# Two usual pairs in place of four in the first gated block, and a re-ordered output stage

## The chip, the core and the metric

The kernel runs on one core of one Trainium2 chip. The metric is the device time of one execution in microseconds. The engines of the core are TensorE (PE in the profile, with PEld for its weight loads), VectorE (DVE), ScalarE (ACT), GpSimd (POOL) and SyncE (SP), which issues DMAs. Each engine works through its own instructions in order; semaphores make one engine wait for another or for a DMA. PE writes its products into PSUM, which has eight banks of 512 fp32 columns.

## What is computed

Two equal layers, each an attention part and a gated part with a residual around each. There are 2048 tokens of 448 features, 16 heads of 28 and 1792 hidden features.

```python
def _A_ref(x, wqkv, wo):
    q, k, v = ...                       # x @ wqkv, by heads
    scores = einsum("bhqd,bhkd->bhqk", q, k) * (Dh ** -0.5)
    o = einsum("bhqk,bhkd->bhqd", softmax(scores), v)
    return heads_together(o) @ wo

def _B_ref(x, w_gate, w_up, w_down):
    h = sigmoid(x @ w_gate) * (x @ w_up)
    return h @ w_down

x = A_x
x = x + _A_ref(_layernorm(x), A_wqkv, A_wo)
x = x + _B_ref(_layernorm(x), B_w_gate, B_w_up, B_w_down)
x = x + _A_ref(_layernorm(x), A_wqkv, A_wo)
x = x + _B_ref(_layernorm(x), B_w_gate, B_w_up, B_w_down)
```

## The kernel before

A layer runs through four stages: `project` (queries, keys, values), `attend`, `out_project` (the product with `wo` and the residual) and `gated`. The tokens stand in 16 tiles of 128, and four tiles make a block of 512. In the products of these stages every fp32 operand is split into two fp16 parts, high and low, and a product is three matmuls: high by high, high by low, low by high. The order of the instructions on each engine is written out by hand; nothing is scheduled later.

**The output stage (`out_project`, L1365).** For a token tile, `products` (L1373) runs nine matmuls of 448 columns into one bank, and `tails` (L1376) adds the last 64 features of the contraction; two tiles' second tail matmuls use halves of the array. `add` (L1387) adds the result into `x` on DVE. The tiles go in groups of 6, 4, 4 and 2. Block 0 is normalised meanwhile: `stats` (L493) on DVE and POOL, `scale` (L319) on DVE, then `turn_raw` (L511) transposes its four tiles on PE into the banks 4 to 7, ACT copies them to SBUF, and the nine `half_steps` (L385) make from them the fp16 operands `xwide` and `xshort`: sums and differences of quarters of the block, as a product in the manner of Strassen needs them.

**The gated stage (`gated`, L1463).** The outer loop runs over four blocks, the inner one over seven pairs of hidden tiles (`seq`). `gate_and_up` (L1610) computes for one pair the gate and the up product, 78 matmuls of 256 columns, in two PSUM tiles `chain` and two `side`. ACT copies partial sums out of `chain` (L1625); DVE adds `side` to them (L1641, `c11_c22`), after which PE goes on accumulating in `side` (`c12`, the last ten matmuls of the pair). Between these pieces stand six slots, `along(0)` to `along(5)`; `portions` (L1801) says how many steps of a queue `steps` are taken in which slot of which pair. The third slot, `along(2)`, is the last before `c11_c22`.

**The down product.** From block 1 on it runs a block late, in seven products a pair (`pieces`, L1556), each of six matmuls of 224 columns (L1552); `Operands` (L1495) makes their fp16 operands from the hidden values on ACT and DVE. For block 0, the first `USUAL` pairs take another way: `hidden` (L1695) splits the hidden values as they are, and `down` (L1587) runs 24 matmuls of 448 columns (L1600 to L1602) into four banks of their own, one pair later. `add_usual` (L1605) adds these banks into `x` at the pairs that `AFTER_USUAL` names. `load_usual` (L1439) loads the weights of this form, `load_dn` (L1447) those of the other, for block 0 only the pairs that are not usual.

**Blocks 1 to 3 before their use.** A block goes through a queue of steps (`steps`, L373). `norm_two` makes the statistics of two tiles (DVE) and their factors (POOL); `lift` scales a tile on ACT; `square` transposes it in squares of 32 on DVE. The last `square` also runs `store` (L342), four DMAs to a scratch in DRAM, and `gather` (L354), two DMAs back that bring the features onto the partitions (`xraw`). The nine `half_steps` follow; the first, `r11`, reads the gathered tile on DVE (L403) and on ACT (L411). All DMAs of `store` and `gather`, the usual weights and the first down weights are issued by SP, in order; the gate and up weights of a pair (1.6 MB, L1437) by POOL when PE has ended the pair two before.

Of the kernel before, what the change touches and what calls it, by code (L numbers as in the profile page):

```python
# [21 lines left out]
D = 448  # L22
# [3 lines left out]
NT = S // P  # L26
NB = 4
TB = NT // NB
# [28 lines left out]
N_SUMS = 25  # L57
DN = D // 2

AFTER_USUAL = ((0, 5), (0, 5), (1, 0), (1, 2))  # L60
N_DN = 8
USUAL = 4
SHORT = ((10, 23, 12), (11, 24, 13), (8, 22, 9))


# [53 lines left out]
def interleaved_layers(ctx: ExitStack, tc: tile.TileContext, x_in, wqkv, wo, w_gate, w_up,  # L119
                       w_down, out):  # L120
    nc = tc.nc
# [10 lines left out]
    banks = {"pool": None, "stack": None}  # L132
# [11 lines left out]
    def psum(tag, name, shape):  # L144
        uid[0] += 1
        return banks["pool"].tile(shape, F32, name=f"{name}_{uid[0]}", tag=tag, bufs=1)
# [4 lines left out]
    def bank(i, name):  # L151
        return psum(f"bank{i}", name, [P, 512])


    x = cpool.tile([P, NT, D], F32, name="x")
# [14 lines left out]
    back = cpool.tile([P, 4], F32, name="back")  # L170
# [92 lines left out]
    class Block:  # L263
# [246 lines left out]

        def turn_raw(self):  # L511
            self.turned = True
            self.turn_banks(4, range(4))
            self.raw = big.get("xraw", [P, 4, W])
            nc.gpsimd.memset(self.raw[64:P, 3, :], 0.0)
            for j in range(TB):
                self.turn(j)
            for kt, pt in self.pt.items():
                n = P if kt < 3 else 64
                nc.scalar.copy(self.raw[0:n, kt, :], pt[0:n])  # L520
            big.put(self.xn)
# [60 lines left out]
    def by_tokens(pm, hi, lo, tail, w, kts=range(4)):  # L582

        for kt in kts:
            if kt == 3:
                nc.tensor.matmul(pm, tail, w[:, 0, 3, :], start=False, stop=False)
                nc.tensor.matmul(pm, tail, w[:, 1, 3, :], start=False, stop=True)
                continue
            nc.tensor.matmul(pm, hi(kt), w[:, 0, kt, :], start=(kt == 0), stop=False)  # L589
            nc.tensor.matmul(pm, hi(kt), w[:, 1, kt, :], start=False, stop=False)  # L590
            nc.tensor.matmul(pm, lo(kt), w[:, 0, kt, :], start=False, stop=False)  # L591
# [114 lines left out]
    def run_fill(fill, n=1):  # L706
        for _ in range(n):
            if fill:
                fill.popleft()()
# [215 lines left out]
    class Measure:  # L925
# [27 lines left out]
        def add(self):  # L953
            kind, t, n = self.rows.popleft()
            m, n = {"o": (3, n), "d": (6, n), "gu": (4, 1024)}[kind]
            v = t[:, 0:n]
            junk = big.get("junk", [P, 2048], BF16)
            nc.vector.tensor_tensor_reduce(junk[:, 0:n], v, v, 1.0, sums[:, m:m + 1],
                                           op0=ALU.mult, op1=ALU.add,
                                           accum_out=self.part[:, 0:1])  # L960
            big.put_next(junk)
            nc.vector.tensor_copy(sums[:, m:m + 1], self.part[:, 0:1])
            if kind == "gu":
                junk = qrt.get("junk", [P, 1024], BF16)
# [29 lines left out]
    class Prepare:  # L994
# [119 lines left out]
        def split(self, raw, kind, j):  # L1114
# [22 lines left out]
            else:  # L1137
                n = N_DN if j < USUAL else N_DN - 1
                t = big.at(self.packs, "pack", [P, N_DN, 2, DN], F16)
                s12, s34 = [qrt.get("sums", [P, 2, DN]) for _ in range(2)]  # L1140
                b11, b12, b21, b22 = [v[:, z, c:c + DN] for z in (1, 0) for c in (0, DN)]
                for to, a, b in ((s12[:, 0], b12, b11), (s12[:, 1], b22, s12[:, 0]),
# [3 lines left out]
                         (t[:, 3:6:2], v[:, 0].rearrange("p (c n) -> p c n", c=2))]  # L1146
                if j < USUAL:
                    parts.append((t[:, 7], b12))
# [8 lines left out]
    class Outputs:  # L1157
# [9 lines left out]
        def hi(self, t):  # L1167
            return lambda kt: self.kt[kt][:, 0, t * P:(t + 1) * P]

        def lo(self, t):  # L1170
            return lambda kt: self.kt[kt][:, 1, t * P:(t + 1) * P]
# [193 lines left out]
    def out_project(outs, gate):  # L1365
        new_banks()
        nc.scalar.activation(warm, warm, AF.Sigmoid)
        nc.scalar.reg_load(gate_scale, back.bitcast(I32)[0:1, 3:4])
        first = Block(0, True)
        steps = deque([first.turn_raw] + first.half_steps())  # L1370
        early = 6

        def products(pm, t):  # L1373
            by_tokens(pm, outs.hi(t), outs.lo(t), None, gate.out, range(3))

        def tails(pms, ts):  # L1376


            for t in ts:
                nc.tensor.matmul(pms[t], outs.tail(t), gate.out[:, 0, 3, :], start=False,  # L1380
                                 stop=False)
            for i, t in enumerate(ts):
                r = slice(64 * (i % 2), 64 * (i % 2) + 64)
                nc.tensor.matmul(pms[t], outs.tail(t, i % 2), gate.out[r, 1, 3, :], start=False,  # L1384
                                 stop=True)

        def add(pm, t):  # L1387
            nc.vector.scalar_tensor_tensor(x[:, t, :], pm, back[:, 1:2], x[:, t, :],
                                           op0=ALU.mult, op1=ALU.add)

        gate.load_gu()
        gate.load_usual()
        pms = {t: bank(t, "op")[:, 0:D] for t in range(early)}
        for t in range(early):
            products(pms[t], t)
        first.begin()
        tails(pms, range(early))
        for t in range(early):
            add(pms[t], t)
            if t < TB:  # L1400
                first.stats(t)
            if t >= TB:
                first.scale(t - TB)
        for j in range(early - TB, TB):
            first.scale(j)
        for ts in (range(6, 10), range(10, 14), range(14, NT)):
            for t in ts:
                pms[t] = bank((6, 7, 0, 1, 2, 3, 4, 5, 0, 1)[t - early], "op")[:, 0:D]
                products(pms[t], t)
                if t >= 10:  # L1410
                    run_fill(steps, {10: 4}.get(t, 1))
            tails(pms, ts)
            for t in ts:
                add(pms[t], t)
        big.put(*outs.kt, gate.out)
        run_fill(steps, 9)
        return first


    class WeightsGated:  # L1420
# [18 lines left out]
        def load_usual(self):  # L1439

            self.usual = [big.get("usual", [P, 2, 4, 2, DN], F16)
                          for _ in range((USUAL + 1) // 2)]
            for p in range(USUAL):
                for i, k in enumerate((3, 5, 0, 7)):
                    nc.sync.dma_start(self.usual[p // 2][:, p % 2, i], dn_parts[k, :, p])

        def load_dn(self, queue=nc.sync):  # L1447
            t = big.get("dn", [P, NP, 2, DN], F16)
            first = USUAL if len(self.products) > NP * (NB - 1) else 0
            queue.dma_start(t[:, first:], dn_parts[self.products.popleft(), :, first:])  # L1450
# [12 lines left out]
    def gated(layer, first, wt, before_next):  # L1463
# [2 lines left out]
        low, high = slice(0, W // 2), slice(W // 2, W)  # L1466

        seq = [(b, p) for b in range(NB) for p in range(NP)]
        blks = [first] + [Block(b, True) for b in range(1, NB)]
        s1, s2 = blks[1].steps(), blks[2].steps()  # L1470
        norms = TB // 2
        ahead = norms + 2 * TB
        steps = deque(s1[:ahead] + s2[:norms] + s1[ahead:] +
                      s2[norms:ahead])
        banks_of = {}


# [65 lines left out]
        def of_block(b):  # L1543
            return range(USUAL if b == 0 else 0, NP)

# [157 lines left out]
        for b, p in seq:  # L1703
# [25 lines left out]
            for i, n in enumerate(portions(b, p)):  # L1729
                at[i].append(lambda n=n: run_fill(steps, n))  # L1730
            for j in range(TB):
                if AFTER_USUAL[j] == (b, p):
                    at[0].append(lambda j=j: add_usual(j))


            if b > 0:
                some = [q for q in (0, 1, 6, 2, 3, 4, 5) if q in of_block(b - 1)]
                for q in some:
                    i = {0: 0, 1: 1, 6: 2, 2: 3, 3: 4}.get(q, 5)
# [28 lines left out]
        b = NB - 1  # L1768
# [10 lines left out]
        for k in TAIL[3:]:  # L1779
            if k == 6:  # L1780
                for j, i in enumerate((0, 2)):
# [4 lines left out]
                    if last:  # L1786
                        t = b * TB + j
# [13 lines left out]
    def portions(b, p):  # L1801

        if b == 0:
            steps = {0: {1: 2, 2: 2, 4: 2, 5: 4}, 2: {1: 1, 2: 1, 5: 1},
                     3: {1: 1, 2: 1, 3: 1, 4: 1, 5: 1}, 4: {1: 1, 2: 1, 3: 2, 4: 2, 5: 2},
                     5: {1: 2, 2: 1}}
        elif b == 1:
            steps = {1: {1: 1, 5: 1}, 2: {5: 1}, 3: {2: 1}, 4: {1: 1, 5: 1}, 5: {1: 1, 5: 1},
                     6: {2: 1}}
        elif b == 2:  # L1810
            steps = {0: {1: 1, 2: 1}, 1: {1: 2, 2: 2, 5: 4}, 3: {5: 1}, 4: {1: 1, 2: 1, 5: 1},
                     5: {1: 1, 2: 1, 5: 1}, 6: {1: 1, 3: 1}}
        else:
            steps = {0: {1: 1, 2: 1}, 1: {1: 2, 2: 2, 5: 2}, 2: {1: 1, 2: 1, 5: 1},
                     3: {1: 1}, 4: {1: 1, 2: 1}, 5: {1: 2, 2: 2}, 6: {1: 2, 2: 2, 5: 2}}
        return [steps.get(p, {}).get(i, 0) for i in range(6)]
# [6 lines left out]
    first = Block(0)  # L1823
# [82 lines left out]
```

## Time and profile before

| | us |
|---|---|
| median of three runs | 1895.12 (1894.42 to 1895.16) |
| span of the profiled execution | 1893.0 |
| output stage of layer 0 | 565.9 to 600.3 |
| block 0 of layer 0's gated stage, pair 0 begins | 600.3 |
| output stage of layer 1 | 1501.7 to 1536.1 |
| block 0 of layer 1's gated stage, pair 0 begins | 1536.1 |

No time of its own is listed for the profiled execution beside its span; the median lies 2.1 us above the span.

In the timelines a row gives the start, the length, the engine, the line, the operation, what it writes and reads, and how many such instructions are merged in it; the brackets at its end give how long the engine had stood idle and who released it. A queue's own rows, with the letter q, are DMAs being issued. Matmuls overlap in the array, so their cost is the step from one start to the next and not the length. In a table of windows each engine has its busy time and, in brackets, its number of instructions; then come the clock of PE, the share of the DMA engines and GB/s. In the list of waits stand the total, the count and the longest. Line numbers are those of the kernel before.

### The profile page before, as it was taken

The numbers are of one execution on the slowest core, as the hardware profiler recorded it, in microseconds if no ns is written. First come the engines' busy times: TensorE is split into PE (matmuls) and PEld (weight loads), VectorE is DVE, ScalarE is ACT, GpSimd is POOL, SyncE is SP. The second block draws the span as 40 slices with busy tenths as digits, with TensorE's granted clock in tenths as the row PEclk, the third lists the DMA queues.
The fourth block names the chain that finished last, engine by engine and source line by source line (L and its number), as shares of the span: only waits on it lengthen the run. The fifth ranks groups of instructions, "written<-read, shape, count | busy, mean of one in ns | idle before, by whom it ended". The sixth has DMA issues, their size and how long they took to land. (4 is left out here: it accounts for less than half of the span.)

```text
span 1893.0 us, 56282 instructions
## 1 busy us (share of the span) xinstructions
PE 1886.5 (100%) x24254; PEld 1323.1 (70%) x24254; DVE 1430.7 (76%) x2835; ACT 1382.7 (73%) x1772; POOL 231.5 (12%) x453
## 2 busy tenths in 40 slices
PE   9999999999999999999999999999999999999999
PEld 4455555555556799999954556667666567999998
DVE  7758989898976688787564487787778676887664
ACT  5569999999993566555345799999999745565541
POOL 3023112222101111111100000000000020121110
PEclk9999999999999999999999999999999999999999
DMA  7676454334323566646734322122120245666553
GB/s 247 194 212 166 132 137 128 107 119 129 103 88 121 192 205 235 231 181 238 251 96 134 90 52 47 32 52 52 31 48 24 67 160 174 218 251 223 208 208 142
DMA packets 110882, 270.86 MB, mean 143 GB/s; under 512 B 13214, under 2 KB 67838, under 8 KB 110496
## 3 DMA queue, kind: packets, MB, share of 16 engines
q0 software_dynamic: 31776, 158.51, 23.4%
q1 hardware_dynamic: 78288, 108.20, 20.3%
q8 instruction: 192, 3.15, 0.7%
q10 hardware_dynamic: 560, 0.46, 0.1%
q14 instruction: 66, 0.54, 0.1%
HBM read 207.88 MB, written 50.85 MB: 137 GB/s over the span
## 5 line engine op out<-in xcount | busy, mean ns | idle before, releaser
L1222 ACT ACTIVATE prob_s<-sc 128x1536 f32<-128x1536 f32 (+1 forms) x657 | 887.9, 1487 | 6.6 <-PE sc L1207 5.9
L1258 PE MATMUL acc<-prob_s,val_s 128*32 128x256 f32 (+3 forms) x7700 | 569.9, 383 | 0.0
L1207 PE MATMUL sc<-qp_s 114*32 114x512 f16 x7868 | 553.2, 379 | 0.0
L579 PEld LDWEIGHTS <-gu_s 128*128 128x128 f16 x4368 | 426.9, 98 | 46.8 <-issue 0.4
L1207 PEld LDWEIGHTS <-qp_s 114*32 114x32 f16 x8192 | 272.7, 95 | 203.4 <-issue 88.3
L1258 PEld LDWEIGHTS acc<-prob_s,val_s 128*32 128x32 f32 x7700 | 272.3, 110 | 142.9 <-issue 13.6
L579 PE MATMUL chain<-xwide_s,gu_s 128*128 128x256 f16 x2016 | 247.5, 273 | 0.0
L1552 PE MATMUL dnp<-dn_s,hparts_s 128*128 128x224 f16 x2016 | 225.2, 259 | 0.0
L1552 PEld LDWEIGHTS <-hparts_s 128*128 128x128 f16 x2016 | 194.0, 98 | 4.4
L1238 DVE SCALAR_TENSOR_TENSOR power_q<-power_q,expo_q 128x512 f32<-128x512 f32 x243 | 168.2, 692 | 8.3
L1625 ACT COPY one_q<-chain 128x256 f32<-128x256 f32 x224 | 82.4, 371 | 121.4 <-PE chain L579 120.8
L1641 DVE TENSOR_TENSOR one_q<-side,one_q 128x512 f32<-128x512 f32 x112 | 72.2, 686 | 101.8 <-PE side L579 101.5
L579 PE MATMUL side<-xshort_s,gu_s 128*128 128x256 f16 x1120 | 140.5, 273 | 0.0
L564 PE MATMUL qkp<-xhl_s,wqk_s 128*128 128x512 f16 x616 | 138.1, 379 | 0.7 <-ACT wqk_s L231 0.2
L564 PEld LDWEIGHTS <-wqk_s 128*128 128x128 f16 x616 | 60.1, 98 | 69.8 <-ACT wqk_s L231 1.1
L1437 POOL DMA_DIRECT2D gu_s<-gu_parts x104 | 56.0, 538 | 430.5 <-PE side L579 424.5
L1287 DVE STREAM_TRANSPOSE oturned_q<-acc 128x512 f32<-128x512 f32 x32 | 22.9, 716 | 97.1 <-PE acc L1258 96.9
L1258 PE MATMUL acc<-power_q,val_s 128*32 128x256 f32 (+3 forms) x300 | 94.2, 396 | 0.0
L579 PE MATMUL side<-xwide_s,gu_s 128*128 128x256 f16 x672 | 91.6, 273 | 0.0
L1505 ACT CAST hparts_s<-hsums_q 128x256 f16<-128x256 f32 (+1 forms) x136 | 65.0, 494 | 30.2 <-DVE hsums_q L1517 20.2
L756 ACT ACTIVATE qkhl_q<-qkp 128x512 f16<-128x512 f32 x56 | 33.2, 593 | 71.9 <-PE qkp L564 68.3
L1652 ACT ACTIVATE one_q<-one_q 128x512 f32<-128x512 f32 x56 | 35.2, 629 | 64.3 <-DVE one_q L1641 64.3
(218 smaller groups left out, 2318.0 us busy)
## 6 DMA issues: line engine op xcount, KB each, us to landing
gu_s<-gu_parts POOLq DMA_DIRECT2D x104, 800.0 KB, 6.0
dn_s<-dn_parts POOLq DMA_DIRECT2D x42, 784.0 KB, 7.8
qp_s<-qk_scr SPq DMA_DIRECT2D x96, 224.0 KB
qk_scr<-qkhl_q SPq DMA_DIRECT2D x56, 256.0 KB
gu_parts<-pack_s POOLq DMA_DIRECT2D x14, 800.0 KB, 3.8
xt_scr<-xs_s SPq DMA_DIRECT2D x48, 224.0 KB
xraw_s<-xt_scr SPq DMA_DIRECT2D x12, 768.0 KB
qp_s<-qk_scr SPq DMA_DIRECT2D x64, 112.0 KB
```

Source lines behind the costliest of these rows:

```text
L564: nc.tensor.matmul(pm, w, x, start=(i == 0), stop=(i == len(terms) - 1))
L579: nc.tensor.matmul(pm, a, x, start=(first and i == 0), stop=(i == len(terms) - 1), skip_group_check=True)
L1207: nc.tensor.matmul(ps[32 * j:32 * j + 32, :], hd.k[:, keys], hd.q[:, qb * W:(qb + 1) * W], start=True, stop=True, tile_position=(0, 32 * j))
L1222: nc.scalar.activation(prob[:, 0:n, :], ps[:, 0:n, :], AF.Exp, scale=exp_scale)
L1238: nc.vector.scalar_tensor_tensor(p, p, c[k], y, op0=ALU.add, op1=ALU.mult)
L1258: nc.tensor.matmul(acc[qb * VC:(qb + 1) * VC, s], v[:, kc % TB, h, :], probs[c * NB + qb][:, s], start=(kc == 0 and a == 0), stop=(kc == N ...
L1437: queue.dma_start(self.gu[-1][m], gu_parts[p, m])
L1505: nc.scalar.copy(to[:, :, 0], a)
L1552: nc.tensor.matmul(pm, a[:, x, t], w[:, p, y], start=(begin and n == 0 and (j == 0 or alone)), stop=(n == 2), skip_group_check=True)
L1625: nc.scalar.copy(to, pm)
L1641: nc.vector.tensor_tensor(one[m], side[m], one[m], op=ALU.add)
L1652: nc.scalar.activation(out, v, AF.Sigmoid, scale=gate_scale)
```

## The change

Three things, in both layers.

- `USUAL` is 2: in block 0 the pairs 2 and 3 take the way of the seven products. `AFTER_USUAL` adds the first two banks at the pairs 3 and 4 of block 0. With it, `load_usual` loads half, `load_dn` five of seven pairs for block 0, from pair 1 on, and the preparation makes one part less for two pairs' down weights.
- The output stage takes the tiles in four groups of four tails. Block 0's tiles 0 to 3 are added and scaled first, and its transposition goes into the banks 2 to 5 behind the products of tiles 8 and 9.
- Block 1's two `norm_two` and four `lift` are made in the output stage, so its queue in the gated stage begins with the four `square`, the store and the gather. `portions` takes them in the second slot of pair 0, and `r11` in the third slot of pair 1. Before, the squares stood in the sixth slot of pair 0 and `r11` in the sixth of pair 2. The steps of block 2 that follow alternate between `lift` and `square`.

```diff
-AFTER_USUAL = ((0, 5), (0, 5), (1, 0), (1, 2))
+AFTER_USUAL = ((0, 3), (0, 4), (1, 0), (1, 2))
 N_DN = 8
-USUAL = 4
+USUAL = 2
...
         def turn_raw(self):
             self.turned = True
-            self.turn_banks(4, range(4))
+            self.turn_banks(2, range(4))
...
-        first = Block(0, True)
+        first, second = Block(0, True), Block(1, True)
         steps = deque([first.turn_raw] + first.half_steps())
-        early = 6
+        early = second.squared()[:TB + TB // 2]
+        pms = {}
...
-        pms = {t: bank(t, "op")[:, 0:D] for t in range(early)}
-        for t in range(early):
-            products(pms[t], t)
+        products(range(6), range(6))
         first.begin()
-        tails(pms, range(early))
-        for t in range(early):
-            add(pms[t], t)
-            if t < TB:
-                first.stats(t)
-            if t >= TB:
-                first.scale(t - TB)
-        for j in range(early - TB, TB):
-            first.scale(j)
-        for ts in (range(6, 10), range(10, 14), range(14, NT)):
-            for t in ts:
-                pms[t] = bank((6, 7, 0, 1, 2, 3, 4, 5, 0, 1)[t - early], "op")[:, 0:D]
-                products(pms[t], t)
-                if t >= 10:
-                    run_fill(steps, {10: 4}.get(t, 1))
-            tails(pms, ts)
-            for t in ts:
-                add(pms[t], t)
+        tails(range(4))
+        for t in range(4):
+            add(t)
+            first.stats(t)
+        products((6, 7), (6, 7))
+        tails(range(4, 8))
+        for t in range(4):
+            first.scale(t)
+        for t in range(4, 8):
+            add(t)
+        products((8, 9), (0, 1))
+        run_fill(steps)
+        for do in early[:2]:
+            do()
+        products((10,), (6,))
+        run_fill(steps, 2)
+        products((11,), (7,))
+        run_fill(steps)
+        tails(range(8, 12))
+        for t in range(8, 12):
+            add(t)
+        for do in early[2:]:
+            do()
+        products((12, 13), (2, 3))
+        run_fill(steps, 3)
+        products((14, 15), (0, 1))
+        run_fill(steps, 9)
+        tails(range(12, NT))
+        for t in range(12, NT):
+            add(t)
         big.put(*outs.kt, gate.out)
-        run_fill(steps, 9)
-        return first
+        return first, second
...
-        steps = deque(s1[:ahead] + s2[:norms] + s1[ahead:] +
-                      s2[norms:ahead])
+        steps = deque(s1[norms + TB:ahead] + s2[:norms] + s1[ahead:] +
+                      [s2[i] for i in (2, 6, 3, 7, 4, 8, 5, 9)])
...
         if b == 0:
-            steps = {0: {1: 2, 2: 2, 4: 2, 5: 4}, 2: {1: 1, 2: 1, 5: 1},
-                     3: {1: 1, 2: 1, 3: 1, 4: 1, 5: 1}, 4: {1: 1, 2: 1, 3: 2, 4: 2, 5: 2},
-                     5: {1: 2, 2: 1}}
+            steps = {0: {1: 4, 5: 2}, 1: {2: 1, 4: 1, 5: 2},
+                     2: {1: 1, 2: 1, 3: 1, 4: 1, 5: 3}, 3: {1: 2}, 4: {1: 2}, 5: {1: 2}}
```

More of the change, by code (lines that the diff above doesn't have):

```diff
@@ L1368, in out_project, with products, tails @@
         nc.scalar.reg_load(gate_scale, back.bitcast(I32)[0:1, 3:4])
-        first = Block(0, True)
+        first, second = Block(0, True), Block(1, True)
         steps = deque([first.turn_raw] + first.half_steps())
-        early = 6
-        def products(pm, t):
-            by_tokens(pm, outs.hi(t), outs.lo(t), None, gate.out, range(3))
-        def tails(pms, ts):
+        early = second.squared()[:TB + TB // 2]
+        pms = {}
+        def products(ts, banks):
+            for t, i in zip(ts, banks):
+                pms[t] = bank(i, "op")[:, 0:D]
+                by_tokens(pms[t], outs.hi(t), outs.lo(t), None, gate.out, range(3))
+        def tails(ts):
             for t in ts:
@@ L1385, in tails, with add @@
                                  stop=True)
-        def add(pm, t):
-            nc.vector.scalar_tensor_tensor(x[:, t, :], pm, back[:, 1:2], x[:, t, :],
+        def add(t):
+            nc.vector.scalar_tensor_tensor(x[:, t, :], pms[t], back[:, 1:2], x[:, t, :],
                                            op0=ALU.mult, op1=ALU.add)
@@ L1468, in gated @@
         seq = [(b, p) for b in range(NB) for p in range(NP)]
-        blks = [first] + [Block(b, True) for b in range(1, NB)]
+        first, second = first
+        blks = [first, second] + [Block(b, True) for b in range(2, NB)]
         s1, s2 = blks[1].steps(), blks[2].steps()
```

## The prediction

> **What bounds the kernel now.** I read the busy table of the page first, then the list of what TensorE (PE) waited for, then the timelines of the two changed stages, in layer 0 (565.9 to about 678 us) and in layer 1.
>
> ```profile
> span 1893.0 us, 56282 instructions
> ...
> PE 1886.5 (100%) x24254; PEld 1323.1 (70%) x24254; DVE 1430.7 (76%) x2835; ACT 1382.7 (73%) x1772; POOL 231.5 (12%) x453
> ```
>
> ```profile
> PE still L261 <- DVE warm L179: 1.3, 1, 1.3
> PE turn L508 <- DVE xn_s L320: 0.8, 1, 0.8
> PE qkp L564 <- ACT wqk_s L231: 0.2, 1, 0.2
> PE qkp L564 <- DVE xhl_s L543: 0.2, 1, 0.2
> ```
>
> These four rows are all of PE's waits on another engine, and all lie in the kernel's first 20 us. In the output stage and the gated block PE never waits: it runs one matmul after another, so their issue spacing sets the end there. Two consequences: work taken from PE is gained in full, but there is no wait to remove; and any wait that the change puts in front of PE is lost in full.
>
> **Part 1: fewer PE columns.** The pairs 2 and 3 of block 0 leave the usual form (24 matmuls of 448 columns a pair) for seven products of six 224-column matmuls (42 a pair).
>
> ```profile
> 1552.08 1.25 PE L579 MATMUL side<-xshort_s,gu_s 128*128 128x256 f16 x10
> 1557.71 1.47 PE L579 MATMUL chain<-xwide_s,gu_s 128*128 128x256 f16 x12
> ```
>
> ```profile
> 687.17 1.31 PE L1552 MATMUL dnp<-dn_s,hparts_s 128*128 128x224 f16 x12
> 688.32 1.47 PE L579 MATMUL chain<-xwide_s,gu_s 128*128 128x256 f16 x12
> ```
>
> Between the first two rows stand 10 matmuls of 256 columns (1.09 us, the step from 614.05 to 615.14 in a fence below) and one usual pair: 5.63 - 1.09 = 4.54 us. Twelve of 224 columns take 1.15 us, so 42 take 4.03. Gain: 0.51 us a pair, times two pairs and two layers: 2.06 us. That is the whole of what PE can gain, since the gate and up products do not change.
>
> What these pairs cost elsewhere: each drops two casts and two subtractions of 512 for seven casts, four sums and seven subtractions of 256. Row that covers it, from a pair that already works so:
>
> ```profile
> 675.61 1.29 DVE L1641 TENSOR_TENSOR one_q<-side,one_q 128x512 f32<-128x512 f32 x2 [0.92 <-PE side L579]
> ```
>
> VectorE (DVE) stands 0.92 us idle there; the new pairs 3 and 4 add a transposition (0.55) and an accumulator's addition (0.6), 1.15 in all, and the 0.28 us worked out in Part 3 absorbs the rest. I take 0; without this cover some 0.3 us a pair. Down weights of five pairs in place of three are loaded after pair 1 and not 3, on SyncE's (SP) queue behind the gather of Part 3, and are due only in block 1; the weights' preparation in attention makes two pieces fewer on DVE, which PE does not await. Both 0.
>
> **Part 2: the re-ordered output stage.** All matmuls stay, in four groups of tails of four token tiles each (before 6, 4, 4, 2).
>
> ```profile
> 576.13 1.30 PE L1380 MATMUL op<-wout_s,ot_s 128*128 128x448 f16 x6
> 577.36 0.74 PE L1384 MATMUL op<-wout_s,ot_s 64*128 64x448 f16 x6
> ...
> 584.86 0.92 PE L1380 MATMUL op<-wout_s,ot_s 128*128 128x448 f16 x4
> ...
> 586.19 0.36 PE L589 MATMUL op<-wout_s,ot_s 128*128 128x448 f16 x1
> ...
> 587.90 1.91 PE L508 MATMUL turn<-ident,xn_s 128*128 128x128 f32 x16
> ```
>
> ```profile
> 577.76 0.68 DVE L1388 SCALAR_TENSOR_TENSOR x<-op,back,x 128x448 f32<-128x448 f32 x1 [8.00 <-PE op L1384]
> ...
> 583.58 0.65 DVE L1388 SCALAR_TENSOR_TENSOR x<-op,back,x 128x448 f32<-128x448 f32 x1
> ...
> 585.17 1.35 DVE L320 TENSOR_SCALAR xn_s<-x,mv,rs 128x448 f32<-128x448 f32 x3
> 586.43 2.46 DVE L1388 SCALAR_TENSOR_TENSOR x<-op,back,x 128x448 f32<-128x448 f32 x4
> ```
>
> A group of four tails takes 1.33 us (584.86 to 586.19), two tiles' products 18 x 0.19 = 3.4. New order on PE from 576.13: tails to 577.46, products 6 and 7 to 580.9, tails to 582.2, products 8 and 9 to 585.6, then the transpositions. They now write banks 2 to 5, so bank 5 needs tile 5 added. DVE begins two tails (0.38) earlier, at 577.38; four additions with statistics take 5.82 (577.76 to 583.58), four scalings 1.7, two additions 1.25: 586.2. PE waits about 0.35 us for it, 0.7 in both layers. Bounds: 0 and 0.7 a layer (one addition more). The block's start moves with it: pair 0 begins at S0 = 600.28 + 0.35 = 600.63.
>
> Block 1's statistics (3.0 us on DVE), GpSimd's (POOL) eight small operations and ScalarE's (ACT) four scalings (2.8) now stand between block 0's transposition and its operands.
>
> ```profile
> 565.90:600.30 34.40, 34.40 (x197) 17.66 (x194) 23.24 (x43) 8.24 (x15) 3.64 (x9) 1.00 0.37 116
> ```
>
> In this stage DVE (23.24 of 34.40 us) and ACT (8.24) have room. Following their queues, block 0's wide operands are done by about 598 and its short ones by 601; PE needs the first at S0, the last in S0 + 5.2. Cost 0; DVE is the thinner cover, and a late operand would cost PE its delay one for one. On POOL's queue these stand ahead of weight loads that wait for pair 0's end anyway.
>
> **Part 3: block 1's trip through memory.** Its squares (four transpositions), the store (four DMAs on SP) and the gather (two) move from the end of pair 0 to its second slot, and the gather's first user, r11, from pair 2's last slot to pair 1's third. There r11's cast stands on ACT ahead of the sigmoids, and its subtractions on DVE ahead of the sums of side and one; both engines work in order. PE's last ten matmuls of pair 1 need these sums.
>
> ```profile
> 600.28 1.49 PE L579 MATMUL chain<-xwide_s,gu_s 128*128 128x256 f16 x12
> ...
> 608.81 1.47 PE L579 MATMUL chain<-xwide_s,gu_s 128*128 128x256 f16 x12
> ...
> 614.05 1.25 PE L579 MATMUL side<-xshort_s,gu_s 128*128 128x256 f16 x10
> 615.14 1.26 PE L579 MATMUL chain<-xshort_s,gu_s 128*128 128x256 f16 x10
> 616.23 1.26 PE L579 MATMUL side<-xshort_s,gu_s 128*128 128x256 f16 x10
> 617.32 0.35 PE L1600 MATMUL dnp<-usual_s,hhl_q 128*128 128x448 f16 x1
> ```
>
> ```profile
> 610.18 2.22 DVE L316 STREAM_TRANSPOSE xs_s<-lifted_q 128x448 f32<-128x448 f32 x4
> ...
> 615.21 1.29 DVE L1641 TENSOR_TENSOR one_q<-side,one_q 128x512 f32<-128x512 f32 x2 [1.32 <-PE side L579]
> ```
>
> ```profile
> 631.50 0.76 DVE L403 TENSOR_TENSOR t_q<-xraw_s 128x256 f32<-128x256 f32 x2
> ```
>
> When the data must be there: the second sum ends at 616.50, the second five matmuls start at 616.23 + 0.55, so the sums may start 0.28 late, 6.68 after the pair's start (608.81). Before them stand r11's subtractions, 0.76. So the gather must land 5.92 into pair 1, which starts 8.53 after S0: at S0 + 14.45.
>
> When the store starts: the last four additions begin as the last tails end (about S0 - 0.1, as at 577.76 against 577.36) and take 2.4, the squares 2.22: S0 + 4.5. The trip has 9.9 us. What it takes today:
>
> ```profile
> 65.58 3.43 SPq L349 DMA_DIRECT2D xt_scr<-xs_s  x4
> 73.73 0.38 SPq L357 DMA_DIRECT2D xraw_s<-xt_scr  x1
> ```
>
> ```profile
> 79.20 1.14 ACT L218 CAST xhl_s<-xraw_s 128x512 f16<-128x512 f32 x2 [4.75 <-DMA xraw_s<-xt_scr]
> ```
>
> ```profile
> 612.43 4.28 SPq L349 DMA_DIRECT2D xt_scr<-xs_s  x4
> 619.52 0.39 SPq L357 DMA_DIRECT2D xraw_s<-xt_scr  x1
> ```
>
> ```profile
> 1548.28 3.18 SPq L349 DMA_DIRECT2D xt_scr<-xs_s  x4
> ```
>
> ```profile
> 1567.24 0.71 ACT L411 CAST xwide_s<-xraw_s 128x256 f16<-128x256 f32 x2 [0.27 <-DMA xraw_s<-xt_scr]
> ```
>
> Two landings are seen, because an engine waited for them: 79.20 - 65.58 = 13.6 us, and 1567.24 - 1548.28 = 19.0 in layer 1, where the store met a weight load. From parts: the shorter store here (612.43 to 619.52, 7.1) with the gather of 73.73 (5.5) makes 12.6. None is near 9.9. In the new place the store starts while no weight load runs, as at 65.58, so I take 13.6: PE waits 13.6 - 9.9 = 3.7 us in each layer, 7.4 together; bounds 2.7 (12.6) and 9.1 (19.0) a layer. What is behind it: ACT's sigmoids and DVE's products of pair 1; PE then has a usual pair (4.54) to run, in which they catch up, so nothing more is late, and pair 3's weight load slips as PE does.
>
> The Trainium skill (DMA: Bandwidth & Descriptors, Anatomy of one DMA) fits a transfer with 2.0 us plus its bytes at 436 GB/s; with that, 0.9 MB out and 0.8 MB back would be an estimated 7.9 us, the wait would vanish and the sum be 1893.8. The trace's 13.6 disagrees.
>
> **Sum**, against the profiled span: 1893.0 - 2.06 + 0.7 + 7.4 = 1899.0, 6.0 more. The median of the runs lies 2.1 above that span, so 1895.1 + 6.0 = 1901.1 us.
>
> **Rivals.** (a) The trip fits into 9.9 us: not slower. For it: the SP queue has eight loads fewer ahead; a gather whose store meets nothing may beat 12.6. Against: no row does. It decides at 9.9: -2.06 + 0.7, 1893.8. (b) The collision of layer 1 stays: there the trip is 19.0 and the wait 9.1: -2.06 + 0.7 + 3.7 + 9.1 = +11.4, 1906.5. For it: the row itself; against: the store leaves some 7 us earlier, ahead of that load. (c) The new wait lets PE's clock fall back.
>
> ```profile
> 1.25 4.87 PE L261 MATMUL still<-still_q 128*128 128x512 f16 x11 [1.25 <-DVE warm L179]
> ...
> 10.54 0.59 PE L261 MATMUL still<-still_q 128*128 128x512 f16 x2
> 10.97 0.50 PE L626 MATMUL sums<-first_sums,ones 128*128 128x1 f32 x4
> ```
>
> At the start 11 matmuls of 512 need 4.87 us, later two need 0.43 (10.54 to 10.97): eleven at that pace are 2.4, so a cold spell costs about 2.5 us; 5.0 in two layers, 1906.1. Against: a wait of 3.7 may be too short. The Trainium skill (TensorE: Matmul & The Clock Gate, Part 1) lets the clock fall after an idle window of about 3.4 us that runs free of the kernel; by that, waits above 3.4 are at the threshold.
>
> **How the numbers follow.** Forecast 0.55, (a) 0.15, (b) 0.13, (c) 0.12; 0.05 for a gain that I do not see. A measurement of this kernel tells about 0.2% (3.8 us) from no change: (a) is within it, and so is the forecast's low end (12.6 gives 1899.0 and a little less falls inside), 0.05. So faster 0.05, same 0.20, slower 0.75. The range takes in (a) to (b): 1893.5 to 1906.5; the forecast's own is 1898 to 1904.
>
> **What would show it.** A row of ACT or DVE released by the gather in pair 1 of block 0, at L411 or L403, in both layers; a PE wait on DVE of 2.5 to 5 us before that pair's last ten matmuls; about 0.35 at the transpositions; a usual-form count of 96 matmuls a layer halved to 48. The prediction is wrong if PE still waits for nothing in pair 1, if the store leaves earlier than 4 us into pair 0, or if PE waits in pairs 2 to 6.

## The result, and the profile after

| | before | after |
|---|---|---|
| median of 11 runs, us | 1894.94 (1894.27 to 1896.11) | 1900.38 (1897.88 to 1903.09) |
| span of the profiled execution, us | 1893.0 | 1897.4 |

The ratio after to before is 1.0024 (95% interval 1.0017 to 1.0032): slower by 5.4 us. The profiled execution after took 1899.11 us and had the full clock, as 5 of the 11 runs did; it explains 4.4 us. The other six show a granted clock of 0.999 over the run, which comes below.

The list of PE's waits after has three rows beyond the kernel's first 20 us that the list before does not have (total, count, longest):

```profile
PE side L579 <- DVE one_q L1654: 4.1, 2, 2.1
...
PE turn L508 <- DVE x L1391: 0.5, 2, 0.3
...
PE vp L589 <- DVEq L901: 0.4, 1, 0.4
```

The last lies at 116.3 us, in the products for the values of layer 0, which the change leaves alone; before, PE loses 0.15 us there, so it counts for 0.2. The other two come twice, once a layer. The first, in the timelines of SP, ACT, DVE and PE of layer 0 (lines 1552 to 1641 of the kernel before are lines 1565 to 1654 here):

```profile
605.57 3.01 SPq L349 DMA_DIRECT2D xt_scr<-xs_s  x4
...
611.78 0.39 SPq L357 DMA_DIRECT2D xraw_s<-xt_scr  x1
```

```profile
617.79 0.71 ACT L411 CAST xwide_s<-xraw_s 128x256 f16<-128x256 f32 x2 [2.42 <-DMA xraw_s<-xt_scr]
```

```profile
617.79 0.76 DVE L403 TENSOR_TENSOR t_q<-xraw_s 128x256 f32<-128x256 f32 x2 [2.90 <-DMA xraw_s<-xt_scr]
```

```profile
609.56 1.47 PE L579 MATMUL chain<-xwide_s,gu_s 128*128 128x256 f16 x12
...
615.89 1.25 PE L579 MATMUL chain<-xshort_s,gu_s 128*128 128x256 f16 x10
619.20 1.30 PE L579 MATMUL side<-xshort_s,gu_s 128*128 128x256 f16 x10 [2.06 <-DVE one_q L1654]
```

Read it upward: PE's last ten matmuls of pair 1 wait for DVE's sums, these stand behind r11's subtractions, and those and ACT's cast begin in the same instant, 617.79, when the gather has landed. From the store (605.57) the trip took 12.2 us. PE's step from 615.89 to 619.20 is 3.31 us, of which ten matmuls need 1.09: 2.2 us lost. Layer 1 repeats it to a hundredth, though its parts are others (12.2 us from 1543.70 to 1555.93):

```profile
1543.70 3.01 SPq L349 DMA_DIRECT2D xt_scr<-xs_s  x4
1551.28 0.39 SPq L357 DMA_DIRECT2D xraw_s<-xt_scr  x1
```

```profile
1555.93 0.76 DVE L403 TENSOR_TENSOR t_q<-xraw_s 128x256 f32<-128x256 f32 x2 [2.91 <-DMA xraw_s<-xt_scr]
```

The second wait, on PE and DVE of the output stage:

```profile
585.69 0.73 PE L508 MATMUL turn<-ident,xn_s 128*128 128x128 f32 x3
586.69 1.50 PE L508 MATMUL turn<-ident,xn_s 128*64 128x128 f32 x12 [0.27 <-DVE x L1391]
```

```profile
583.27 2.19 DVE L320 TENSOR_SCALAR xn_s<-x,mv,rs 128x448 f32<-128x448 f32 x4
585.38 2.44 DVE L1391 SCALAR_TENSOR_TENSOR x<-op,back,x 128x448 f32<-128x448 f32 x4
```

A transposition is 0.109 us after the one before it (1.91 us for 16 in the rows before, with 0.27 for the last). From the starts of the single matmuls PE lost 0.19, 0.48 and 0.03 us here, 0.70 in all and 0.75 in layer 1. Summed over the output stage and block 0, the steps between PE's matmuls exceed the normal ones by 3.09 us in layer 0 and 3.15 in layer 1, 0.12 of each at the start of pair 5. So -2.06 + 6.24 = +4.2, against +4.4 of the span. The third row adds 0.2, and the waits of the first 20 us are 0.4 shorter: nothing large is left unexplained.

### The profile page after: what moved, and what is told of

Same layout as the page of the kernel before. It is cut to its first block, busy times and chain, and to the rows that moved or that the text cites. A ratio compares the mean times of both kernels' runs of the same rounds, so it can differ in the third digit from the quotient of the medians.

```text
span 1897.4 us, 56456 instructions
## 1 busy us (share of the span) xinstructions
PE 1886.2 (99%) x24326; PEld 1328.5 (70%) x24326; DVE 1442.8 (76%) x2867; ACT 1391.0 (73%) x1792; POOL 235.9 (12%) x453
## 3 DMA queue, kind: packets, MB, share of 16 engines
q8 instruction: 192, 3.15, 0.7%
## 5 line engine op out<-in xcount | busy, mean ns | idle before, releaser
L1565 PE MATMUL dnp<-dn_s,hparts_s 128*128 128x224 f16 x2184 | 245.9, 259 | 0.0
L1565 PEld LDWEIGHTS <-hparts_s 128*128 128x128 f16 x2184 | 210.2, 98 | 5.1
L1518 ACT CAST hparts_s<-hsums_q 128x256 f16<-128x256 f32 (+1 forms) x152 | 71.5, 485 | 35.1 <-DVE hsums_q L1530 23.6
```

The costliest lines, as they stand in the source:

```text
L1518: nc.scalar.copy(to[:, :, 0], a)
L1565: nc.tensor.matmul(pm, a[:, x, t], w[:, p, y], start=(begin and n == 0 and (j == 0 or alone)), stop=(n == 2), skip_group_check=True)
```

## The experiments

All but the last two are set against runs of the kernel before, taken beside them on the same chip: medians of 1895.38 us for the first four, 1894.95 for the next three, 1894.94 for three more.

### r11 at the end of pair 1

```diff
-            steps = {0: {1: 4, 5: 2}, 1: {2: 1, 4: 1, 5: 2},
+            steps = {0: {1: 4, 5: 2}, 1: {5: 4},
```

> One edit on the changed kernel: in block 0's pair 1 all four steps r11, t1, t2 and t3 are taken in the sixth slot, behind the pair's last sums of side and one, in place of r11 in the third, t1 in the fifth and two in the sixth. Store and gather stay where they are. Theory (the wait for the gather at r11 is what costs): the gather lands at about 12.2 us after the store as before, DVE reaches r11 some 0.5 us after that, and PE's wait of 2.27 us in pair 1 goes in both layers: 4.5 us less than the changed kernel's span of 1897.4, about 1892.8 us, and the median about 0.5 us under the kernel before; the granted clock is 1.000 in all runs. Rival (DVE is short of time in pairs 1 to 6, whatever r11 waits for): the wait moves to a later pair and the span stays within 1 us of 1897.4.

Measured: 1896.66 us (11 runs), ratio 1.001 (1.0001 to 1.0019), profiled span 1894.3. The wait for the sums is gone in both layers, as it had to be if the gather held them up. The time saved is 3.1 us and not 4.4, since the list of PE's waits has a new row:

```profile
PE chain L579 <- DMA gu_s<-gu_parts: 1.4, 2, 1.1
```

```profile
623.44 0.83 PE L579 MATMUL chain<-xwide_s,gu_s 128*128 128x256 f16 x6 [0.29 <-DMA gu_s<-gu_parts]
```

By the steps it costs 0.45 us in layer 0 and 1.27 in layer 1: pair 2's weights are late. POOL's timeline tells why, here of the kernel after, and below it of the kernel before:

```profile
612.34 0.19 POOL L291 TENSOR_SCALAR rs<-mv 128x2 f32<-128x2 f32 x1 [18.23 <-DVE mv L288]
...
616.08 0.22 POOL L304 TENSOR_SCALAR off<-off 128x2 f32<-128x2 f32 x1
616.76 1.28 POOL L1449 DMA_DIRECT2D gu_s<-gu_parts  x2 [0.46 <-DMA xraw_s<-xt_scr]
```

```profile
608.73 1.28 POOL L1437 DMA_DIRECT2D gu_s<-gu_parts  x2 [2.08 <-PE side L579]
```

Before, POOL issued these loads as soon as pair 0 let the buffers go. After, the norm steps of block 2, taken in pair 0's last slot, stand ahead of them on POOL's queue; they wait for DVE until 612.34, and the loads leave 15.7 us into pair 0 and not 8.4. In the kernel after, the wait for the gather hides that.

### The additions between the scalings, and both edits

```diff
         for t in range(4):
             first.scale(t)
-        for t in range(4, 8):
-            add(t)
+            add(t + 4)
```

> One edit on the changed kernel: in the output stage the additions of tiles 4 to 7 stand between the four scalings on DVE (scaling, addition, scaling, addition and so on) and not behind them. Theory: bank 5 is then free after two scalings and two additions, about 585.8 us, when PE arrives at the transpositions, so of PE's 0.70 us of waits there at least 0.5 us goes in each layer, and the store leaves earlier by as much, but so does r11's place: the wait for the gather stays at 2.2 to 2.4 us. Span about 1896.2. Rival (the transpositions wait for the scaled tiles, not for bank 5): the 0.70 us stay and the span is 1897.4.

Measured: 1899.06 us (11 runs), ratio 1.0016 (1.0007 to 1.0025), span 1895.0. PE no longer waits at the transpositions at all; the wait in pair 1 is 1.50 us in layer 0 and 2.19 in layer 1. The shorter one is not owed to the edit: the trip took 11.5 us there in this execution (604.74 to 616.24), as it also did in one of the later profiles of the kernel after.

> The edits of the two runs before together: r11 late, and the additions between the scalings. If both waits are independent the gains add: 4.5 and 1.2 us, span about 1891.6 us, and the median 1.5 to 1.9 us (0.1%) under the kernel before, which is the gain of the 224-column products (2.06 us) with next to no wait left. If less than 1 us under the kernel before, a wait is left that I have not named.

Measured: 1894.98 us (11 runs), ratio 0.9997 (0.9988 to 1.0006), span 1894.5: level with the kernel before. Both waits are gone. The one for pair 2's weights is 0.70 us in layer 0 and 1.80 in layer 1: 0.49 until the first of the two loads lands, and 1.30 until the second does (it lands at 1560.67 and PE goes on at 1560.72, though the list names DVE there). And 0.7 us more than before is lost in the first 20 us of this execution (1.5 in place of 0.8 for the first `xn_s`). From 1893.0 - 2.06 + 0.24 = 1891.2, the span with the small wait at pair 5 alone, 1891.2 + 2.5 + 0.7 = 1894.4.

### Two usual pairs alone

The kernel before with the first part of the change only.

```diff
-AFTER_USUAL = ((0, 5), (0, 5), (1, 0), (1, 2))
+AFTER_USUAL = ((0, 3), (0, 4), (1, 0), (1, 2))
...
-USUAL = 4
+USUAL = 2
```

> One part of the change alone: the kernel before with two usual pairs in place of four and the accumulators added at pairs 3 and 4, but with its own output stage, its own places of block 1's norms and steps. Theory: pair 3 of block 0 now has no usual product behind it, 8.5 us of PE, while DVE's steps there sum to some 12.6 us (sums and products of the pair 3.1, operands 3.7, five half steps 5.2, an addition 0.6) and in pair 4 to some 9.8: PE waits for DVE about 5 us in each layer, and the kernel is 6 to 10 us slower than before. Rival (DVE has room, as the operands cost nothing): 2.06 us faster than before.

Measured: 1903.62 us (5 runs), ratio 1.0046 (1.0032 to 1.0059), span 1901.1. Its list of PE's waits begins:

```profile
PE side L579 <- DVE two_q L1648: 3.2, 6, 0.9
...
PE chain L579 <- ACT one_q L1625: 2.6, 4, 0.9
```

By the steps PE loses 5.1 us in block 0 of layer 0 and 5.5 in layer 1: -2.06 + 10.5 = +8.4, against +8.1 of the span. The waits lie in the pairs 4 to 6 (643.7 to 666.5). The operands of the pairs that work the other way do not fit beside block 1's half steps, eight of which stand in the pairs 3 and 4 here, and block 2's scalings on ACT behind them. In the kernel after, the half steps stand in the pairs 1 and 2. Their earlier place, which the moves into the output stage allow, is what makes the first part worth its 2.06 us, as far as the timelines tell; it was not tested by itself.

### The norm steps behind the loads

Block 2's two norm steps go from pair 0's last slot to pair 1's second, so that POOL issues pair 2's loads first; once with the two edits above, once in the kernel after alone (the second's edit is shown; in the first, pair 1 reads `{1: 2, 5: 4}`).

```diff
-            steps = {0: {1: 4, 5: 2}, 1: {2: 1, 4: 1, 5: 2},
+            steps = {0: {1: 4}, 1: {1: 2, 2: 1, 4: 1, 5: 2},
```

> This is the kernel after with three edits: r11 at the end of pair 1, the additions between the scalings, and block 2's two norm steps moved from pair 0's last slot to pair 1's second, so that on POOL's queue pair 2's gate/up loads stand ahead of them and not behind. Theory (the wait that r11's move uncovered is POOL's order): the loads are issued near 609.7 us instead of 616.5, both PE waits on gu_s at the start of pair 2 (0.70 and 1.30 us in the kernel with the first two edits) vanish, and what is left is the change's own gain: 1893.0 - 2.06 + 0.24 = 1891.2 span, about 1893.0 a run, some 2 us under the kernel before. Rival (the loads are late because the gather and the down weights use the DMA engines at the same time): issued early they meet the gather instead, the wait stays or becomes one of r11 on the gather, span about 1893.2, run 1895.

Measured: 1898.14 us (11 runs), ratio 1.0015 (1.0006 to 1.0025), span 1894.4. The theory held in its first half (no wait on `gu_s` is left) and failed in the second: DVE's statistics now stand ahead of pair 1's sums and cost 1.24 us a layer, and ACT's copies of pair 2 come 0.57 us late in each layer, behind r11's casts.

> The kernel after with only the norm steps moved behind pair 2's loads on POOL's queue. Theory: the late load is hidden behind the longer wait for the gather, so nothing is gained by it alone; PE's waits in pair 1 stay at 2.3 us a layer or grow by up to 1 us (400 KB of weights then move while the gather does), span 1897.4 to 1899.4. Rival (the gather's landing is late because POOL is busy or because of what is queued on POOL): the wait shrinks, span 1895 or less.

Measured: 1910.71 us (5 runs), ratio 1.008 (1.0066 to 1.0094), span 1907.5. Both theories were wrong by far. Its timelines of POOL, SP, DVE and PE in layer 0:

```profile
609.12 1.28 POOL L1449 DMA_DIRECT2D gu_s<-gu_parts  x2 [15.38 <-PE side L579]
```

```profile
605.21 3.01 SPq L349 DMA_DIRECT2D xt_scr<-xs_s  x4
611.55 0.39 SPq L357 DMA_DIRECT2D xraw_s<-xt_scr  x1
```

```profile
620.28 0.76 DVE L403 TENSOR_TENSOR t_q<-xraw_s 128x256 f32<-128x256 f32 x2 [3.05 <-DMA xraw_s<-xt_scr]
```

```profile
615.53 1.25 PE L579 MATMUL chain<-xshort_s,gu_s 128*128 128x256 f16 x10
621.69 2.29 PE L579 MATMUL side<-xshort_s,gu_s 128*128 128x256 f16 x10 [4.90 <-DVE one_q L1654]
623.78 0.58 PE L1613 MATMUL dnp<-usual_s,hhl_q 128*128 128x448 f16 x1
```

The loads leave 7 us earlier in the block than in the kernel after, ahead of the gather, and the gather lands 8.7 us after its issue and not 6.0 (in layer 1 8.8 and not 4.7): the trip is 15.1 us, in layer 1 16.4. I had taken the loads for 400 KB; they are two of 800. The wait is 5.1 us (6.4 in layer 1). And the ten matmuls behind it take 2.09 us from start to start in place of 1.09. The windows of PE's clock (the third column from the right):

```profile
609.00:616.50 7.50, 7.50 (x71) 6.72 (x69) 4.75 (x13) 3.68 (x9) 1.82 (x4) 1.00 0.99 308
616.50:621.60 5.10, 0.29 (x3) 0.10 (x2) 2.01 (x7) 0.71 (x2) 2.61 (x8) 0.94 0.81 243
621.60:624.00 2.40, 2.31 (x11) 1.62 (x11) 2.30 (x7) 1.41 (x3) 0.63 (x1) 0.50 0.00 0
624.00:632.00 8.00, 8.00 (x55) 5.30 (x54) 6.17 (x15) 3.70 (x8) 0.53 (x1) 0.97 0.59 205
```

Right after the wait the granted clock is 0.50. So POOL's late loads, a flaw that cost 0.45 to 1.8 us a layer once it was uncovered, had kept the gather's way free.

### The store five microseconds later

```diff
-            steps = {0: {1: 4, 5: 2}, 1: {2: 1, 4: 1, 5: 2},
+            steps = {0: {3: 4, 5: 2}, 1: {2: 1, 4: 1, 5: 2},
```

> The kernel after with the squares, the store and the gather moved from pair 0's second slot to its fourth, behind the sums of side and one on DVE: the store starts near S0 + 9.5 instead of S0 + 4.5. Theory (PE waits for the trip's length less the room it has, one for one): the wait in pair 1 grows from 2.3 to about 7.2 us a layer, span 1897.4 + 9.8 = 1907.2. For the clock: if the wait is what lets PE's clock fall in about half of the runs of the kernel after, a wait of 7 us does it in every run, the window behind the wait shows a granted clock below 1.00 in both layers, and 2 us a layer come on top: run near 1913. Rival: the clock's fall has nothing to do with this wait, it stays as frequent as in the kernel before, and the run is near 1909. Rival to the first: the gather is not what sums wait for, and the time moves by less than 3 us.

Measured: 1911.47 us (4 runs, all at a clock of 0.996 or 0.997), ratio 1.0088 (1.0072 to 1.0103), span 1909.8. Its timelines of SP, POOL and DVE, and the windows ahead of, in and behind the wait in layer 0:

```profile
610.32 3.01 SPq L349 DMA_DIRECT2D xt_scr<-xs_s  x4
617.45 0.39 SPq L357 DMA_DIRECT2D xraw_s<-xt_scr  x1
```

```profile
618.43 1.28 POOL L1449 DMA_DIRECT2D gu_s<-gu_parts  x2 [0.46 <-PE chain L579]
```

```profile
622.24 0.76 DVE L403 TENSOR_TENSOR t_q<-xraw_s 128x256 f32<-128x256 f32 x2 [5.69 <-DMA xraw_s<-xt_scr]
```

```profile
611.00:617.90 6.90, 6.65 (x61) 5.97 (x61) 5.26 (x14) 3.48 (x9) 3.32 (x8) 1.00 0.68 137
617.90:623.60 5.70, 0.28 (x3) 0.10 (x1) 1.36 (x4) 0.71 (x2) 1.87 (x4) 0.90 0.83 283
623.60:626.00 2.40, 2.35 (x11) 1.57 (x11) 2.29 (x6) 1.41 (x3) 0.54 (x1) 0.50 1.02 415
```

The store leaves 9.5 us into pair 0, and from it to the first use pass 11.9 us. PE waits 5.6 us in pair 1, and 1.3 at its start for pair 0's products, which the squares hold up on DVE: 6.9, near the 7.2 expected. It is one for one: pair 1 starts 1.3 us late, so the trip has 14.45 + 1.3 - 9.5 = 6.2 us, and 11.9 - 6.2 = 5.7. Behind the wait the clock is 0.50, in both layers. And POOL's loads, here issued 1.0 us behind the gather (2.0 in layer 1), leave it at 4.8 us (5.0).

### Pair 2's loads from SP

```diff
-        def used_gu(self):
+        def used_gu(self, queue=nc.gpsimd):
...
-                self.load_gu(nc.gpsimd)
+                self.load_gu(queue)
...
-            wt.used_gu()
+            wt.used_gu(nc.sync if (b, p) == (0, 0) else nc.gpsimd)
```

> The kernel with r11 at the end of pair 1 and the additions between the scalings, and pair 2's gate/up loads issued by SP, behind the gather on its queue, in place of POOL, behind the norm steps. Theory (two transfers contend: 1.6 MB of weights issued before the gather make it 2.9 us longer, issued too late they are not there at pair 2): behind the gather the weights are issued near 612.6 us, 3.9 before POOL issued them, the gather lands as before (12.2 us after the store), both PE waits on gu_s (0.70 and 1.30) vanish and nothing takes their place: span 1893.0 - 2.06 + 0.24 = 1891.2, run near 1893.0, every run but one in ten at a clock of 1.0. Rival (the loads from SP share the engines with the gather's packets wherever they are queued): the gather lands 2 to 3 us later, ACT's casts of r11 hold up the copies of pair 2 as in the kernel with the norm steps late (0.57 us a layer): span 1892.5, run 1894.3.

Measured, with r11 late and the additions between: 1893.08 us (11 runs, 1892.68 to 1894.08), ratio 0.999 (0.9981 to 0.9999), span 1891.1; every run at the full clock. SP's timeline:

```profile
604.86 3.02 SPq L349 DMA_DIRECT2D xt_scr<-xs_s  x4
611.07 0.39 SPq L357 DMA_DIRECT2D xraw_s<-xt_scr  x1
611.51 0.53 SPq L359 DMA_DIRECT2D xraw_s<-xt_scr  x1
612.13 1.53 SPq L1448 DMA_DIRECT2D gu_s<-gu_parts  x2
613.72 0.43 SPq L1461 DMA_DIRECT2D dn_s<-dn_parts  x1
```

Apart from 0.12 us a layer at the start of pair 5, PE waits for nothing in the output stage or block 0. This kernel is faster than both, than the one before by 1.9 us (0.1%).

> The same two edits with POOL's loads left on POOL, but only one of block 2's two norm steps ahead of them (the other goes to pair 1's first slot). POOL issues pair 2's loads near 614.4 us in place of 616.6. Theory: 2.2 us earlier is more than the 0.70 and 1.30 us that they were late, and the statistics that go to pair 1 (1.45 us of DVE) fit where DVE stood idle for ACT's casts (1.23 and 1.27 us): no PE wait left, span 1891.2 to 1891.8, run near 1893.3. Rival: loads and gather contend for the 2 us that they now overlap, the weights land no earlier, waits of 0.5 to 1 us a layer stay, span 1892.5 to 1893, run near 1894.5.

Here the norm steps stand in `{0: {1: 4, 5: 1}, 1: {0: 1, 5: 4}}`. Measured: 1894.68 us (11 runs), ratio 0.9996 (0.9987 to 1.0005), span 1892.7: between theory and rival. Layer 0's wait is gone; in layer 1 POOL issues 9.3 us behind the store's start and not 11.4, but the loads land only 0.4 us earlier in the block, and PE still waits 1.35 us (0.12 and 1.23) where it waited 1.80. There most of the earlier issue bought nothing, as the rival has it.

> The kernel after with only pair 2's gate/up loads moved to SP, behind the gather. Theory (an early load delays the gather only if it is issued before it): the wait in pair 1 stays at 2.3 us a layer and the span at 1897.4 (run 1898.9 to 1900.4), unlike the norm steps moved alone, where it was 5.1 and 6.4. Rival (any earlier load delays the gather, whatever its place): the wait grows by 2 to 3 us a layer, clock below 1.0 in all runs, run 1906 to 1910.

Measured: 1899.32 us (10 runs), ratio 1.0022 (1.0013 to 1.0032), span 1896.8. The trip is 12.4 us (605.27 to 617.65), PE's wait 2.4 and 2.2 us. Behind the gather, the same 1.6 MB do not delay it, although they are issued 4 us earlier in the block than in the kernel after (3 in layer 1).

### The kernel after, twice more

> The kernel after, profiled once more, for an execution whose clock is below 1.0. Theory (a wait of 2.3 us in pair 1 lets PE's clock fall in some executions): such a profile shows a granted clock near 0.5 for some 2 us behind the wait in pair 1 of one layer or of both, matmuls of 256 columns 214 ns apart there in place of 109, and nowhere else in the output stage or block 0; span 1898.6 or more. Rival: the clock falls at another place, or the span is longer for another reason. With a clock of 1.0 the look only repeats the profile: span 1896 to 1898, the same two waits.

> The same kernel and the same question, a second execution: about half of them had a clock below 1.0.

Both executions had a clock of 0.999 (1899.92 and 1899.57 us, spans 1898.2 and 1897.9). The first one's windows around the wait, two in layer 0 and two in layer 1, then the second one's (behind the comma stands PE's busy time):

```profile
615.29:618.71 3.42, 1.45 (x15) 1.14 (x13) 1.53 (x4) 0.85 (x3) 2.19 (x5) 1.00 0.82 242
618.71:622.12 3.41, 3.41 (x15) 1.97 (x14) 3.31 (x9) 1.42 (x4) 1.08 (x2) 0.50 1.02 419
1553.95:1557.37 3.42, 1.94 (x18) 1.58 (x17) 0.65 (x2) 0.82 (x3) 2.54 (x6) 1.00 0.99 322
1557.37:1560.78 3.41, 2.65 (x18) 1.75 (x18) 3.31 (x9) 1.47 (x4) 0.63 (x2) 1.00 1.03 417
```

```profile
614.61:618.02 3.41, 2.25 (x21) 1.86 (x19) 1.27 (x3) 1.08 (x3) 2.66 (x7) 1.00 1.00 311
618.02:621.43 3.41, 3.27 (x22) 2.09 (x22) 3.31 (x10) 1.41 (x3) 1.39 (x3) 1.00 0.89 334
1553.27:1556.68 3.41, 1.29 (x12) 1.00 (x11) 1.94 (x4) 1.26 (x4) 1.70 (x3) 1.00 1.05 372
1556.68:1560.10 3.42, 3.42 (x14) 1.72 (x13) 3.17 (x10) 1.43 (x5) 0.54 (x1) 0.50 1.01 412
```

In each, one layer's wait (2.1 and 2.3 us) is followed by a stretch at half the clock, and the other layer's (2.4 and 1.5 us) is not. Of the 11 runs after, the five at the full clock average 1898.8 us, the six at 0.999 1901.1: a run with the fall is about 2.3 us longer, of which 3.41 us at half the clock make 1.7. The trips behind the four waits are 12.2, 12.4, 11.5 and 12.3 us, so that those of the first profile agreed to a hundredth was chance.

When a wait is followed by the fall can be read from the clock records of the traces. Within an execution the clock changes only at instants that lie whole multiples of 3.413 us apart: in the first of these two it rises to 1.00 at 4.31 us and falls at 618.71, 180 such steps later; in the second 7.03 and 1556.68 lie 454 steps apart; in the two kernels with waits of 5 us it is 180 and 181. The windows above are such steps. By the profile's count PE stands idle for 1.97 us (3.42 - 1.45) in the step ahead of the first fall, and for 2.12 in that ahead of the second. The waits that no fall follows are divided by the border of two steps: 1.48 and 0.76 us, 1.16 and 0.14. In all fourteen profiles, up to the kernel's end, no step with 1.60 us or less was followed by a fall, and each with 1.97 or more that began at the full clock was. So a wait of 2 us costs clock or not by where it falls among these steps.

The fall follows the wait in the other runs too: 0.999 or less stood in 6 of 11 runs after, 7 of 11 with only the additions moved, 6 of 10 with only the loads on SP, but in 4 of the 55 runs of the five kernels with r11 late. The kernel before showed it in 9 of the 69 runs beside these; where, no profile here tells.

## Why the prediction came out right, and where it was wrong

The forecast was 1901.1, the median is 1900.38. The mechanism was right; two of the sum's terms were off to opposite sides, and a rival that the sum left out is part of the time. Of the signs that I had named, the rows released by the gather came in both layers, and 48 matmuls of the usual form a layer; but the wait in pair 1 (2.2 us) lies under the 2.5 to 5 that I had named, and PE waits 0.12 us at pair 5, where any wait was to count against the prediction.

**Part 1, 2.06 us gained: right.** The fastest experiment shows the gain without the waits: 1893.0 to 1891.1 is 1.9, and 2.06 - 0.24 (the small wait at pair 5) is 1.8. "Some 0.3 us a pair" without cover was wrong: the first part alone loses 5 us a layer.

**Part 2, 0.35 us a layer: mis-sized.** It is 0.70 and 0.75, about the upper bound. The start on DVE was right (583.2 worked out, 583.27 seen), but the four scalings took 2.11 us from first start to the addition's (583.27 to 585.38), not 1.7: the fourth waited until 584.64 for POOL's factor of its tile, which the working left out, and took 0.79 us in place of 0.51. So tile 5's addition ended some 0.4 us later than worked out, and the third transposition also waited, 0.19 us, for that of tile 4. That it is the additions' place on DVE that counts is shown: placed between the scalings, they cost nothing.

**Part 2's sentence on POOL: wrong.** "On POOL's queue these stand ahead of weight loads that wait for pair 0's end anyway" was said of block 1's operations. Block 2's norm steps, moved to pair 0's last slot by the same change, were not put on POOL's queue at all in the working, and they hold the loads until 616.8. It cost nothing in this kernel because a longer wait lay over it, and by keeping 1.6 MB out of the gather's way it made that wait shorter.

**Part 3, 3.7 us a layer: right in place, mis-sized.** The store was to leave 4.5 us into pair 0 (601.04): it did, 4.53. The room of 9.9 us holds too: 12.2 - 9.9 = 2.3, and 2.2 was lost. The trip was 12.2 us, not 13.6, and below my lower bound of 12.6; that bound took the shortest store and the only gather that the trace showed, but store and gather were 6.21 and 6.01 us in layer 0 and 7.58 and 4.65 in layer 1. The Trainium skill's fit (DMA: Bandwidth & Descriptors, Anatomy of one DMA), by which I had estimated 7.9 us, came out too short in both layers; the page gives it for a DMA that GpSimd issues, and these are SyncE's.

**The rivals.** (a), no wait, did not come. (b), the collision: not in this kernel, but the loads put ahead of the gather made it (15.1 and 16.4 us of trip). (c), the clock: I gave it 0.12 beside the forecast, at 2.5 us in both layers; it is real, 1.7 us in about every second run, in one layer of each of the two that were profiled. I held a wait of 3.7 us for perhaps too short, and 2.1 was enough. The Trainium skill (TensorE: Matmul & The Clock Gate, Part 1) has the clock fall after an idle window of about 3.4 us that runs free of the kernel. That the fall comes and goes between runs at equal waits agrees with a free-running window, and so do the steps of 3.413 us; that 1.97 us of idling within a step suffices does not agree with a whole idle window of 3.4. Waits of 5 us and more brought it in every run.

Put together: -2.06 + 4.44 (predicted 7.4) + 1.45 (0.7) + 0.24 (0) = +4.1 in an execution at the full clock, and 2.3 us more in six of eleven, which puts the median at +5.4. The closeness to +6.0 is partly luck: in place of waits of 3.7 us a layer came 2.2 us a layer and, in half of the runs, 1.7 us of slow clock in one of them.

## What to carry to other kernels

When work is moved forward so that another engine's operand comes over DRAM, compare the whole trip, store to first use, with the room between the two slots, and put the first user where an in-order engine has nothing urgent behind it. Walk every queue past which a step is moved, also for its neighbours in the same slot, and ask of each load both when it must land and which transfer it will meet: too late cost 0.45 to 1.8 us a layer here, too early 3 to 4 us of trip, behind the gather nothing. Where PE never waited, price a new wait of 2 us at its length and, for some of the runs, at 1.7 us of slow clock on top.

## What the runs showed that I had not expected

- A PE wait of 2.1 us let the granted clock fall to 0.50 for 3.41 us (618.71 to 622.12) in some executions and not in others, by how the wait lay among steps of 3.413 us: 1.97 us idle within one step was enough, 1.60 was not. Waits of 5.0 us and more did so in every run.
- 1.6 MB of loads issued 2.4 us ahead of a gather of 0.9 MB lengthened it from 6.0 to 8.7 us; issued right behind it on the gather's own queue, they left it as it was (trip 12.4 us). On POOL's queue 1.0 us behind it, with the store later, they did so too (gather 4.8 us): the order protects it, not the queue.
- Taking a wait away uncovered the next one under it twice: 4.4 us of waits in the two layers became 1.7 us of another, and 2.5 us, in the kernel with both edits, 3.6.
